# Where the Q, K and V columns are put in (dim, head) order: in the weights, or in the copy out of PSUM

## The chip, the core and the metric

The kernel runs on one NeuronCore of a Trainium2 chip. Its engines are TensorE (PE, matmuls and transposes into PSUM), VectorE (DVE), ScalarE (ACT), GpSimd (POOL) and SyncE (SP, which here only issues DMAs). Each engine runs its instructions in the order in which they were written for it, and waits for others by semaphores. The metric is the time of one execution in microseconds on the device.

## What is computed

One transformer block on 2048 positions of 576 columns, in bf16:

```
S, D, H, Dh, F = 2048, 576, 32, 18, 4608
y   = layernorm(x)                                   # no affine part, eps 1e-5
qkv = (y @ wqkv).reshape(S, 3, H, Dh)                # column = t*576 + head*18 + dim
q, k, v = qkv[:, 0], qkv[:, 1], qkv[:, 2]
idx = pos[:, None] - 2 * arange(8)                   # 8 earlier positions, two apart; masked below 0
logits[h, s, w] = dot(q[s, h], k[idx[s, w], h]) * 18 ** -0.5
attn = softmax(logits over w)
o[s, h] = sum over w of attn[h, s, w] * v[idx[s, w], h]
h1  = x + o.reshape(S, D) @ wo
out = h1 + gelu(layernorm(h1) @ w1 + b1) @ w2 + b2   # tanh form of gelu
```

## The kernel before

The positions are cut into 16 tiles so that partition p of tile j holds position 16 p + j. The eight keys that a query needs then lie in eight tiles of the same parity, and `ORDER` takes the even tiles first and the odd ones after, each from the highest down. `kwin[e]` and `vwin[e]` are windows of eight slots, one for each tile of parity e.

**Layout.** VectorE computes the scores: one product of the window with q (line 445), then sums over the 18 dims in halving steps (line 451), which need the columns in (dim, head) order, so that 32 heads lie next to each other. The weights come in (head, dim) order. In this kernel they are loaded as they are into a raw tile, `wraw` (lines 201 and 205, K by the ScalarE queue, V and Q by SP), and fifteen copies, `perm` (line 290), one for each of Q, K, V and each of the five blocks of 128 rows, put them into `wqkv_sb` in (dim, head) order. Blocks 1 and 3 are copied by ScalarE, blocks 0, 2 and 4 by VectorE. The queries, keys and values then leave TensorE in the wanted order.

**The first stage, for each tile n** (`front`): load x; statistics on VectorE (`ln1a`: lines 314, 315, and the variance with eps in line 318); the inverse root by a power on GpSimd (`ln1r`, line 322); normalisation (`ln1b`) on VectorE for the first eight tiles (line 354) and on ScalarE for the others (line 357, with a factor from GpSimd, line 349); transposition (`t1`), for the first eight tiles by TensorE (line 329) and a ScalarE copy out of PSUM (`t1e`, line 373), for the others by a transposing DMA (line 371). Then three chunks, `c{n}K`, `c{n}V`, `c{n}Q`: each ten matmuls (two halves of 288 columns, five blocks of rows, line 394) into one PSUM buffer of two banks, and one ScalarE copy, `e{n}K` and so on (line 406), into the window or a query tile. K chunks of the first eight tiles come first. The chunks of Q, K, V need all five `perm` copies of their third. The PSUM pool `pm` has three buffers, for transposes, chunks, projections and MLP units together.

**Attention and the rest.** VectorE needs eight K slots and a query for its first product (`p1a`), and all eight V slots for the weighted sum (line 486). Its outcome is transposed, projected by `wo` (line 564), added to x, normalised again, transposed again (`t2`, `t3`), and goes into the MLP, eight groups of two tiles: units of 36 matmuls with w1 (line 630), gelu on ScalarE (line 641), and matmuls with w2 (line 667). The last tiles' K and V slots are refilled, shifted by a row, through DRAM (lines 426, 427, 520, 522).

**Order.** All work is a list of tasks with an engine, an expected cost, tasks that they come after, a priority, and buffers that they take and give. A planner, `Weaver.run`, puts them in one order, always the task with the earliest start, by priority where starts tie; that fixes each engine's instruction order before the kernel runs. A changed cost or dependence can therefore reorder work far behind it. DMA tasks (`load`, `bulk`) carry a size; the planner holds bulk weights back while its model of the queue is full. The weights w2 (18 loads) wait for all `perm` copies, since their tile takes the place of `wraw`.

Of the kernel before, what the change touches and what calls it, by code (L numbers as in the profile page):

```python
# [8 lines left out]
ACT = mybir.ActivationFunctionType  # L9
ALU = mybir.AluOpType  # L10
AX = mybir.AxisListType
BF16 = mybir.dt.bfloat16
# [3 lines left out]
class Weaver:  # L16
# [74 lines left out]
def kernel(  # L91
# [46 lines left out]
    FH = FT // 2  # L138
    w1_sb = wpool.tile([P, KC, F // 2], BF16, name="w1_sb")
    wo_sb = wpool.tile([P, KC, HALF], BF16, name="wo_sb")  # L140
    hn_bufs = [wpool.tile([P, KC, 2 * P], BF16, name="hnT0")]
    b1_raw = wpool.tile([FT, P], BF16, name="b1_raw")
    b1_sb = wpool.tile([P, FT], F32, name="b1_sb")
    ident = wpool.tile([P, P], BF16, name="ident")
    b2_bc = wpool.tile([P, D], BF16, name="b2_bc")
# [7 lines left out]
    early_cm = tc.tile_pool(name="early", bufs=1)  # L153
    early = early_cm.__enter__()
    wqkv_sb = early.tile([P, KT, 3 * D], BF16, name="wqkv_sb")
    raw_cm = tc.tile_pool(name="raw", bufs=1, side="right")
    raw = raw_cm.__enter__()
    wraw = raw.tile([P, 3, KT, D], BF16, name="wraw")
    zrow = raw.tile([NT, 2 * D], BF16, name="zrow")

    late, w2p = {}, {}

    def late_pool():
        if not late:
# [24 lines left out]
    def bulk(name, fn, kb, after=(), prio=0.0, issue=0.45):  # L189
        add(name, "SP", issue, fn, after, prio, lag=2.0, kb=kb, backlog=SLACK)  # L190
# [6 lines left out]
    def wq_load(eng, t, k0, k1):  # L197
        def fn():
            src = bass.AP(tensor=A_wqkv.tensor, offset=A_wqkv[k0 * P, t * D].offset,
                          ap=[[3 * D, P], [P * 3 * D, k1 - k0], [1, D]])  # L200
            eng.dma_start(out=wraw[:, t, k0:k1, :], in_=src)
        return fn

    def wq_rest(eng, t):
        return lambda: eng.dma_start(out=wraw[0:64, t, 4, :], in_=A_wqkv[512:576, t * D:(t + 1) * D])

    def wo_load(half, dd):
        def fn():
# [15 lines left out]
        return fn  # L224

    def b1_load():
        nc.sync.dma_start(out=b1_raw[:], in_=B_b1.rearrange("(f p) -> f p", p=P))

    def w2_chunk(c):
        def fn():  # L230
            if "w2" not in w2p:
                raw_cm.__exit__(None, None, None)
                pool = ctx.enter_context(tc.tile_pool(name="w2p", bufs=1, side="right"))
                w2p["w2"] = pool.tile([P, FT, D], BF16, name="w2_sb")
            f0, f1 = c * FT // W2C, (c + 1) * FT // W2C
            nc.sync.dma_start(out=w2p["w2"][:, f0:f1, :],
                              in_=B_w2[f0 * P:f1 * P, :].rearrange("(ft p) c -> p ft c", p=P))
        return fn

# [14 lines left out]

    def b2_load():
        nc.sync.dma_start(out=b2_bc[:], in_=B_b2.partition_broadcast(P))
        nc.sync.dma_start(out=kvd[:, 0, :], in_=zrow[:])

    load("b2", b2_load, 150, prio=8.5, issue=0.7, transfers=2)
    load("b1", b1_load, 20, prio=9.0)  # L260
# [5 lines left out]
    for c in range(W1C):  # L266
        for half in range(2):
            for k in range(0, KC, W1K):
                bulk(f"w1{c}{half}{k}", w1_chunk(c, half, k), 295, prio=20 + c)
    perms = [f"perm{t}{kt}" for t in range(3) for kt in range(KT)]  # L270
    for c in range(W2C):
        bulk(f"w2{c}", w2_chunk(c), 295, prio=30 + c, after=perms + ["b2"])


    nc.gpsimd.memset(mhalf[:], -0.5)
# [1 line left out]
    nc.gpsimd.memset(T["x", 0][:, D:DP], 0.0)  # L277
    make_identity(nc, ident[:])
    nc.gpsimd.memset(wqkv_sb[64:128, KT - 1, :], 0.0)
    nc.gpsimd.memset(zrow[:], 0.0)  # L280
    for n in range(1, NT):
        nc.gpsimd.memset(T["x", n][:, D:DP], 0.0)

    for t in range(3):
        for kt in range(KT):
            def perm(t=t, kt=kt, on=None):
                rows = P if kt < KT - 1 else D - kt * P
                src = wraw[0:rows, t, kt, :].rearrange("p (h d) -> p d h", h=H, d=Dh)
                dst = wqkv_sb[0:rows, kt, t * D:(t + 1) * D].rearrange("p (d h) -> p d h", d=Dh, h=H)
                {"ACT": nc.scalar.copy, "DVE": nc.vector.tensor_copy}[on](out=dst, in_=src)  # L290
            on = "ACT" if kt in (1, 3) else "DVE"
            add(f"perm{t}{kt}", on, {"ACT": 1.23, "DVE": 0.65}[on], lambda f=perm, on=on: f(on=on),
                (f"W{t}{'aabbc'[kt]}",) + ((("ln1b0",) if kt == 2 else ()) if t == K else (f"t1e{2 + 2 * t}" if on == "ACT" else f"ln1b{W - 1}",)),
                prio=(-18, -100, -17)[t])

    def b1_turn():
        T["b1T"] = ps_pm.tile([P, 2048], BF16, tag="pm", name="b1T")[:, 0:FT]
        nc.tensor.transpose(T["b1T"], b1_raw[:], ident[0:FT, 0:FT])
# [22 lines left out]
    def ln_rstd(L, n):  # L321
        nc.gpsimd.tensor_tensor(out=L["rs"][:, n, :], in0=L["ve"][:, n, :], in1=mhalf[:], op=ALU.pow)  # L322
# [15 lines left out]
    def front(n):  # L338
# [2 lines left out]

        def ln1a():
            ln_stats(L1, n, T["x", n][:, 0:D])
            ln_var(nc.vector, L1, n, (1.0, EPS))

        def ln1r():
            ln_rstd(L1, n)
            if n >= W:
                nc.gpsimd.tensor_scalar(out=nmr[:, n, :], in0=L1["mv"][:, n, 0:1], scalar1=L1["rs"][:, n, :],
                                        scalar2=-1.0, op0=ALU.mult, op1=ALU.mult)  # L350
# [21 lines left out]
            else:  # L372
                nc.scalar.copy(out=T["xnT", n], in_=T["pt1", n])  # L373

        add(f"ln1a{n}", "DVE", 1.2, ln1a, (f"x{n}",) + (("ln1b0",) if n == 1 else ()), prio=-20 + n if n < W else 0.5 + (n - W) // 4)
        add(f"ln1r{n}", "POOL", 0.6 if n < W else 1.1, ln1r, (f"ln1a{n}",), prio=-20, lag=0.1 if n < W else 1.0)
        add(f"ln1b{n}", "DVE" if n < W else "ACT", 0.45 if n < W else 0.7, ln1b, (f"ln1r{n}",), prio=-20 + n)
        freed = [m for m in range(LENT, n) if n < 2 * LENT and region(m) == region(n)][-1:]
        room = [f"t1e{m}" for m in range(LENT) if not freed and LENT <= n < 2 * LENT]
# [4 lines left out]
        else:  # L384
            load(f"t1e{n}", lambda: t1e(True), 164, [f"ln1b{n}"] + room, prio=-20 + n, issue=1.2, lag=3.0)

        def chunk(t):
            def fn():
                pq = ps_pm.tile([P, 2, 512], F32, tag="pm", name="pq")
                T["pq", n, t] = pq  # L390
                for half in range(2):
                    c0 = t * D + half * HALF
                    for kt in range(KT):
                        nc.tensor.matmul(pq[:, half, 0:HALF], lhsT=T["xnT", n][:, kt, :],  # L394
                                         rhs=wqkv_sb[:, kt, c0:c0 + HALF],
                                         start=(kt == 0), stop=(kt == KT - 1))
            return fn

        def evict(t):
            def fn():  # L400
                if t == Q:
                    T["q", n] = wpool.tile([P, D], BF16, tag="q", name="q", bufs=NQ)
                    dst = T["q", n][:]
                else:
                    dst = (kwin if t == K else vwin)[e][:, s, :]
                nc.scalar.copy(out=dst.rearrange("p (a c) -> p a c", a=2), in_=T["pq", n, t][:, :, 0:HALF])  # L406
            return fn

        under = [m for m in range(LENT, min(n, 2 * LENT))
                 if region(m) * DP < (s + 1) * D and s * D < (region(m) + 1) * DP]  # L410
        for r, t in enumerate((K, V, Q)):
            first = t == K and n < W
            add(f"c{n}{'QKV'[t]}", "PE", 1.24, chunk(t), [f"t1e{n}"] + [f"perm{t}{kt}" for kt in range(KT)],
                prio=-50 + n if first else -25 if n == 0 and t == Q else -24 + n if t == V and n < W else -10 + n + 0.2 * r,
                take=("pm", f"pq{n}{t}"), lag=0.3)
            lent = []
            if e and t == K:
                lent = [f"t1e{m}" for m in range(LENT)] + [f"c{m}{c}" for m in under for c in "QKV"]
# [198 lines left out]
    def mlp(g):  # L617
# [39 lines left out]
        for i, (a, half) in enumerate(passes):  # L657
            n = ns[a]

            def piece(u, a=a, n=n, half=half):  # L660
                def fn():
                    if u == 0:
                        T["po", n, half] = ps_po.tile([P, HALF], F32, tag="po", name="po")
                    for q in range(2):
                        for r in range(2):
                            ft = r * FH + 2 * u + q
                            nc.tensor.matmul(T["po", n, half][:], lhsT=T["hT", g, u][:, r, q, a * P:(a + 1) * P],  # L667
                                             rhs=w2p["w2"][:, ft, half * HALF:(half + 1) * HALF],
                                             start=(u + q + r == 0), stop=(u == UN - 1 and q + r == 2))
                return fn  # L670

# [61 lines left out]
```

## Time and profile before

| | |
|---|---|
| median of 3 runs | 389.82 us (389.81 to 389.87) |
| profiled execution | 389.9 us, span 388.1 us |
| TensorE busy | 373.1 us, 96% of the span |
| VectorE busy | 297.1 us, 77% |
| ScalarE busy | 220.5 us, 57% |
| GpSimd busy | 37.2 us, 10% |
| clock granted to TensorE | 1.000 |

The times of the text are microseconds from the start of the span. A row of the timeline has start, duration, engine, line, operation, and what it writes and reads with partitions x elements; in square brackets how long the engine had been idle before it and what ended that. Merged rows end in the number of instructions, and their duration reaches from the start of the first to the end of the last.

### The profile page before, as it was taken

Reading aid. Unit: us, or ns where it says so; the run is one execution under the profiler, and the core shown is the slowest. Engines: PE = TensorE matmul, PEld = TensorE weight load, DVE = VectorE, ACT = ScalarE, POOL = GpSimd, SP = SyncE. Lnnn points to the kernel's source line nnn. Section 1 sums busy time; section 2 is a strip of 40 time slices with the busy share of each in tenths; the row PEclk is TensorE's granted clock in tenths of the full one; section 3 lists DMA queues with packets and bytes.
Section 4 is the critical chain, followed back from the end, with each engine's and each line's share of the span. In section 5 each row is a group of like instructions: output and inputs, shape, how many; then the busy total and the mean of one; then the engine's idle time right before and its main releaser. Section 6 shows DMA issues by size and latency. Waiting matters only on the chain.

```text
span 388.1 us, 10761 instructions
## 1 busy us (share of the span) xinstructions
PE 373.1 (96%) x4607; PEld 305.2 (79%) x4607; DVE 297.1 (77%) x559; ACT 220.5 (57%) x447; POOL 37.2 (10%) x65
## 2 busy tenths in 40 slices
PE   2889999999899999999999999999999999999996
PEld 1667877788777887887788878887888788778875
DVE  5999999999999999999999998989976952000000
ACT  4697767688914974188227823790487068306700
POOL 6455010101001000001100010110011011000000
PEclk9999999999999999999999999999999999999999
DMA  8988899887232402127333214222312432100000
GB/s 264 277 165 227 213 212 272 254 255 235 57 83 51 105 19 61 33 63 63 70 77 73 61 48 94 63 47 76 78 37 43 108 64 21 29 15 19 2 15 17
DMA packets 63968, 38.48 MB, mean 99 GB/s; under 512 B 39520, under 2 KB 63904, under 8 KB 63920
## 3 DMA queue, kind: packets, MB, share of 16 engines
q1 hardware_dynamic: 63296, 37.13, 40.4%
q8 instruction: 36, 0.59, 0.7%
q10 hardware_dynamic: 624, 0.66, 0.5%
q14 instruction: 12, 0.10, 0.1%
HBM read 22.28 MB, written 6.52 MB: 74 GB/s over the span
## 4 chain that ended last, share of the span: by engine, by line
PE 74%; DVE 12%; issue 1%; ACT 1%; DVEq 0%; ACTq 0%
PE po L667 37%; PE pm L630 33%; PE pw L564 4%; DVE prod L445 3%; DVE prod L451 2%; DVE prod L486 1%; ACT hT L641 1%; DVE prod L492 1%; DVE l_st L314 1%; DVE h L577 1%; DVE hb L590 1%; DVE half L438 0%; DVE prod L496 0%; DVE half L439 0%; DVE lg L458 0%
## 5 line engine op out<-in xcount | busy, mean ns | idle before, releaser
L641 ACT ACTIVATE hT<-pm,b_sb 128x256 bf16<-128x256 f32 x288 | 111.9, 482 | 82.1 <-PE pm L630 81.8
L630 PE MATMUL pm<-hnT,w_sb 64*128 64x256 bf16 x2592 | 144.5, 269 | 0.8 <-ACT hT L641 0.8
L667 PE MATMUL po<-w_sb,hT 128*128 128x288 bf16 x1152 | 143.2, 286 | 0.0
L630 PEld LDWEIGHTS <-w_sb 64*128 64x128 bf16 x2592 | 125.9, 94 | 17.7 <-issue 2.4
L667 PEld LDWEIGHTS <-hT 128*128 128x128 bf16 x1152 | 111.7, 98 | 30.6 <-issue 2.4
L686 DVE TENSOR_TENSOR osb<-po,hb 128x288 bf16<-128x288 f32 x32 | 14.4, 453 | 57.1 <-PE po L667 57.1
L322 POOL TENSOR_TENSOR l_rs<-l_ve,mhalf 128x1 f32<-128x1 f32 x32 | 28.4, 888 | 287.8 <-DVE l_ve L318 287.8
L451 DVE TENSOR_TENSOR prod<-prod 128x2304 bf16<-128x2304 bf16 (+1 forms) x64 | 44.2, 690 | 1.8
L486 DVE TENSOR_TENSOR prod<-vwin,at 128x4608 bf16<-128x4608 bf16 x16 | 40.9, 2554 | 0.4
L445 DVE TENSOR_TENSOR prod<-kwin,q 128x4608 bf16<-128x4608 bf16 x16 | 40.9, 2555 | 0.3
L394 PE MATMUL pq<-wqkv_sb,vwin 128*128 128x288 bf16 x210 | 30.1, 303 | 3.2 <-ACT vwin L373 1.8
L594 ACT ACTIVATE hn<-h,nmr,l_rs 128x576 bf16<-128x576 f32 (+1 forms) x32 | 19.2, 651 | 23.0 <-issue 11.6
L394 PEld LDWEIGHTS <-vwin 128*128 128x128 bf16 x210 | 21.2, 103 | 10.5 <-ACT vwin L373 2.6
L394 PE MATMUL pq<-wqkv_sb,kwin 128*128 128x288 bf16 x210 | 27.2, 286 | 0.0
L394 PEld LDWEIGHTS <-kwin 128*128 128x128 bf16 x210 | 20.3, 98 | 5.4 <-issue 0.5
L492 DVE TENSOR_TENSOR prod<-prod 128x2304 bf16<-128x2304 bf16 x16 | 21.7, 1358 | 0.6
L569 ACT COPY h<-pw 128x576 f32<-128x576 f32 x16 | 10.4, 651 | 19.4 <-PE pw L564 19.4
L564 PE MATMUL pw<-wo_sb,oT 64*128 64x288 bf16 x288 | 20.3, 283 | 0.0
L577 DVE TENSOR_TENSOR h<-h,xr 128x576 f32<-128x576 f32 x16 | 12.0, 752 | 9.6 <-ACT h L569 9.6
L564 PEld LDWEIGHTS <-oT 64*128 64x128 bf16 x288 | 13.5, 94 | 4.5 <-issue 1.4
L406 ACT CAST kwin<-pq 128x576 bf16<-128x576 f32 x16 | 10.2, 648 | 8.5 <-PE pq L394 8.3
L314 DVE BATCH_NORM_STATS2 l_st<-h 128x6 f32<-128x288 f32 x32 | 13.1, 452 | 0.6
(62 smaller groups left out, 238.2 us busy)
## 6 DMA issues: line engine op xcount, KB each, us to landing
w_sb<-in_B_w_dram SPq DMA_DIRECT2D x36, 288.0 KB, 4.7
xr<-in_A_x_dram SPq DMA_DIRECT2D x16, 144.0 KB, 2.3
out_dram<-osb SPq DMA_DIRECT2D x16, 144.0 KB, 1.8
kvd<-kwin SPq DMA_DIRECT2D x14, 144.0 KB, 4.1
kvd<-vwin SPq DMA_DIRECT2D x14, 144.0 KB, 3.7
kwin<-kvd SPq DMA_DIRECT2D x14, 144.0 KB, 2.5
vwin<-kvd SPq DMA_DIRECT2D x14, 144.0 KB, 2.1
wraw<-in_A_wqkv_dram SPq DMA_DIRECT2D x4, 288.0 KB, 4.1
```

Source lines behind the costliest of these rows:

```text
L314: nc.vector.bn_stats(out=st[:, c, :], in_=src[:, c * HALF:(c + 1) * HALF])
L322: nc.gpsimd.tensor_tensor(out=L["rs"][:, n, :], in0=L["ve"][:, n, :], in1=mhalf[:], op=ALU.pow)
L394: nc.tensor.matmul(pq[:, half, 0:HALF], lhsT=T["xnT", n][:, kt, :], rhs=wqkv_sb[:, kt, c0:c0 + HALF], start=(kt == 0), stop=(kt == KT - 1))
L445: nc.vector.tensor_tensor(out=prod[:], in0=kwin[e][:], in1=T["q", n][:].unsqueeze(1).to_broadcast([P, W, D]), op=ALU.mult)
L451: nc.vector.tensor_tensor(out=pv[:, :, 0:b - a, :], in0=pv[:, :, 0:b - a, :], in1=pv[:, :, a:b, :], op=ALU.add)
L486: nc.vector.tensor_tensor(out=prod[:].rearrange("p w (d h) -> p w d h", d=Dh, h=H), in0=vwin[e][:].rearrange("p w (d h) -> p w d h", d=Dh, ...
L492: nc.vector.tensor_tensor(out=prod[:, 0:4, :], in0=prod[:, 0:4, :], in1=prod[:, 4:8, :], op=ALU.add)
L564: nc.tensor.matmul(pw[:, half, 0:HALF], lhsT=T["oT", n][lo:lo + 64, block(c, half), :], rhs=wo_sb[lo:lo + 64, c, :], start=(c == 0), stop= ...
L594: nc.scalar.activation(out=hn_slots[n % 2][:, c0:c1], in_=src, func=ACT.Identity, scale=L2["rs"][:, n, :], bias=nmr[:, n, :])
L630: nc.tensor.matmul(pm[:, half, q, 0:width], lhsT=w1_sb[lo:lo + 64, c, f0:f0 + P], rhs=T["hnT", g][lo:lo + 64, block(c, half), 0:width], st ...
L641: nc.scalar.activation(out=T["hT", g, u][:, half, q, 0:width], in_=T["pm", g, u][:, half, q, 0:width], func=ACT.Gelu_apprx_tanh, bias=b1_s ...
L667: nc.tensor.matmul(T["po", n, half][:], lhsT=T["hT", g, u][:, r, q, a * P:(a + 1) * P], rhs=w2p["w2"][:, ft, half * HALF:(half + 1) * HALF ...
```

## The change

The weights are loaded straight into `wqkv_sb` in (head, dim) order, and the fifteen `perm` copies and `wraw` are gone. The eviction of each chunk now puts the columns from (head, dim) to (dim, head). For that the PSUM buffer of a chunk is laid out so that its two halves meet at the border of the two banks, and the 576 results lie next to each other. Q and K are evicted in the order of the destination, so ScalarE reads PSUM in steps of 18 fp32 elements (72 bytes) and writes contiguously. V is evicted in the order of the source: ScalarE reads contiguously and writes in steps of 32 bf16 elements (64 bytes).

Along with it: the variance of the first eight tiles moves from VectorE's `ln1a` into GpSimd's `ln1r`, with the planner's costs of both changed; the tile of w2 exists from the start, and lends its room to the raw b1 and to a row of zeros, so w2 now waits for their readers in place of the `perm` copies. The expected cost of an eviction stays 0.68.

```diff
+    w2_sb = wpool.tile([P, FT, D], BF16, name="w2_sb")
+    b1_raw = w2_sb[0:FT, 2, 0:P]
-    b1_raw = wpool.tile([FT, P], BF16, name="b1_raw")
...
-    wraw = raw.tile([P, 3, KT, D], BF16, name="wraw")
-    zrow = raw.tile([NT, 2 * D], BF16, name="zrow")
...
-            eng.dma_start(out=wraw[:, t, k0:k1, :], in_=src)
+            eng.dma_start(out=wqkv_sb[:, k0:k1, t * D:(t + 1) * D], in_=src)
...
-        return lambda: eng.dma_start(out=wraw[0:64, t, 4, :], in_=A_wqkv[512:576, t * D:(t + 1) * D])
+        return lambda: eng.dma_start(out=wqkv_sb[0:64, 4, t * D:(t + 1) * D], in_=A_wqkv[512:576, t * D:(t + 1) * D])
...
-            if "w2" not in w2p:
-                raw_cm.__exit__(None, None, None)
-                pool = ctx.enter_context(tc.tile_pool(name="w2p", bufs=1, side="right"))
-                w2p["w2"] = pool.tile([P, FT, D], BF16, name="w2_sb")
...
-        nc.sync.dma_start(out=kvd[:, 0, :], in_=zrow[:])
+        nc.sync.dma_start(out=kvd[:, 0, :], in_=w2_sb[0:NT, 0:2, :].rearrange("p a c -> p (a c)"))
...
-    perms = [f"perm{t}{kt}" for t in range(3) for kt in range(KT)]
     for c in range(W2C):
-        bulk(f"w2{c}", w2_chunk(c), 295, prio=30 + c, after=perms + ["b2"])
+        bulk(f"w2{c}", w2_chunk(c), 295, prio=30 + c, after=("b2", "b1t"))
...
-    nc.gpsimd.memset(zrow[:], 0.0)
+    nc.gpsimd.memset(w2_sb[0:NT, 0:2, :], 0.0)
...
-    for t in range(3):
-        for kt in range(KT):
-            def perm(t=t, kt=kt, on=None):
-                rows = P if kt < KT - 1 else D - kt * P
-                src = wraw[0:rows, t, kt, :].rearrange("p (h d) -> p d h", h=H, d=Dh)
-                dst = wqkv_sb[0:rows, kt, t * D:(t + 1) * D].rearrange("p (d h) -> p d h", d=Dh, h=H)
-                {"ACT": nc.scalar.copy, "DVE": nc.vector.tensor_copy}[on](out=dst, in_=src)
-            on = "ACT" if kt in (1, 3) else "DVE"
-            add(f"perm{t}{kt}", on, {"ACT": 1.23, "DVE": 0.65}[on], lambda f=perm, on=on: f(on=on), ...
...
         def ln1a():
             ln_stats(L1, n, T["x", n][:, 0:D])
-            ln_var(nc.vector, L1, n, (1.0, EPS))
+            if n >= W:
+                ln_var(nc.vector, L1, n, (1.0, EPS))

         def ln1r():
+            if n < W:
+                ln_var(nc.gpsimd, L1, n, (1.0, EPS))
             ln_rstd(L1, n)
...
-        add(f"ln1a{n}", "DVE", 1.2, ln1a, ...
-        add(f"ln1r{n}", "POOL", 0.6 if n < W else 1.1, ln1r, ...
+        add(f"ln1a{n}", "DVE", 1.07 if n < W else 1.2, ln1a, ...
+        add(f"ln1r{n}", "POOL", 0.95 if n < W else 1.1, ln1r, ...
...
         def chunk(t):
             def fn():
-                pq = ps_pm.tile([P, 2, 512], F32, tag="pm", name="pq")
+                pq = ps_pm.tile([P, 1024], F32, tag="pm", name="pq")
                 T["pq", n, t] = pq
                 for half in range(2):
                     c0 = t * D + half * HALF
+                    p0 = 512 - HALF + half * HALF
                     for kt in range(KT):
-                        nc.tensor.matmul(pq[:, half, 0:HALF], lhsT=T["xnT", n][:, kt, :],
+                        nc.tensor.matmul(pq[:, p0:p0 + HALF], lhsT=T["xnT", n][:, kt, :],
                                          rhs=wqkv_sb[:, kt, c0:c0 + HALF],
                                          start=(kt == 0), stop=(kt == KT - 1))
...
-                nc.scalar.copy(out=dst.rearrange("p (a c) -> p a c", a=2), in_=T["pq", n, t][:, :, 0:HALF])
+                src = T["pq", n, t][:, 512 - HALF:512 + HALF].rearrange("p (h d) -> p h d", h=H)
+                dst = dst.rearrange("p (d h) -> p h d", h=H)
+                if t != V:
+                    src, dst = (ap.rearrange("p h d -> p d h") for ap in (src, dst))
+                nc.scalar.copy(out=dst, in_=src)
...
-            add(f"c{n}{'QKV'[t]}", "PE", 1.24, chunk(t), [f"t1e{n}"] + [f"perm{t}{kt}" for kt in range(KT)],
+            add(f"c{n}{'QKV'[t]}", "PE", 1.24, chunk(t), [f"t1e{n}"] + [f"W{t}{part}" for part in "abc"],
```

More of the change, by code (lines that the diff above doesn't have):

```diff
@@ L155 @@
     wqkv_sb = early.tile([P, KT, 3 * D], BF16, name="wqkv_sb")
-    raw_cm = tc.tile_pool(name="raw", bufs=1, side="right")
-    raw = raw_cm.__enter__()
-    wraw = raw.tile([P, 3, KT, D], BF16, name="wraw")
-    zrow = raw.tile([NT, 2 * D], BF16, name="zrow")
-    late, w2p = {}, {}
+    late = {}
     def late_pool():
@@ L226, in b1_load @@
     def b1_load():
-        nc.sync.dma_start(out=b1_raw[:], in_=B_b1.rearrange("(f p) -> f p", p=P))
+        nc.sync.dma_start(out=b1_raw, in_=B_b1.rearrange("(f p) -> f p", p=P))
     def w2_chunk(c):
         def fn():
-            if "w2" not in w2p:
-                raw_cm.__exit__(None, None, None)
-                pool = ctx.enter_context(tc.tile_pool(name="w2p", bufs=1, side="right"))
-                w2p["w2"] = pool.tile([P, FT, D], BF16, name="w2_sb")
             f0, f1 = c * FT // W2C, (c + 1) * FT // W2C
-            nc.sync.dma_start(out=w2p["w2"][:, f0:f1, :],
+            nc.sync.dma_start(out=w2_sb[:, f0:f1, :],
                               in_=B_w2[f0 * P:f1 * P, :].rearrange("(ft p) c -> p ft c", p=P))
@@ L279 @@
     nc.gpsimd.memset(wqkv_sb[64:128, KT - 1, :], 0.0)
-    nc.gpsimd.memset(zrow[:], 0.0)
+    nc.gpsimd.memset(w2_sb[0:NT, 0:2, :], 0.0)
     for n in range(1, NT):
         nc.gpsimd.memset(T["x", n][:, D:DP], 0.0)
-    for t in range(3):
-        for kt in range(KT):
-            def perm(t=t, kt=kt, on=None):
-                rows = P if kt < KT - 1 else D - kt * P
-                src = wraw[0:rows, t, kt, :].rearrange("p (h d) -> p d h", h=H, d=Dh)
-                dst = wqkv_sb[0:rows, kt, t * D:(t + 1) * D].rearrange("p (d h) -> p d h", d=Dh, h=H)
-                {"ACT": nc.scalar.copy, "DVE": nc.vector.tensor_copy}[on](out=dst, in_=src)
-            on = "ACT" if kt in (1, 3) else "DVE"
-            add(f"perm{t}{kt}", on, {"ACT": 1.23, "DVE": 0.65}[on], lambda f=perm, on=on: f(on=on),
-                (f"W{t}{'aabbc'[kt]}",) + ((("ln1b0",) if kt == 2 else ()) if t == K else (f"t1e{2 + 2 * t}" if on == "ACT" else f"ln1b{W - 1}",)),
-                prio=(-18, -100, -17)[t])
     def b1_turn():
         T["b1T"] = ps_pm.tile([P, 2048], BF16, tag="pm", name="b1T")[:, 0:FT]
-        nc.tensor.transpose(T["b1T"], b1_raw[:], ident[0:FT, 0:FT])
+        nc.tensor.transpose(T["b1T"], b1_raw, ident[0:FT, 0:FT])
     add("b1t", "PE", 0.1, b1_turn, ("b1",), prio=-35, take=("pm", "b1t"), lag=0.3)
@@ L373, in t1e @@
                 nc.scalar.copy(out=T["xnT", n], in_=T["pt1", n])
-        add(f"ln1a{n}", "DVE", 1.2, ln1a, (f"x{n}",) + (("ln1b0",) if n == 1 else ()), prio=-20 + n if n < W else 0.5 + (n - W) // 4)
-        add(f"ln1r{n}", "POOL", 0.6 if n < W else 1.1, ln1r, (f"ln1a{n}",), prio=-20, lag=0.1 if n < W else 1.0)
+        add(f"ln1a{n}", "DVE", 1.07 if n < W else 1.2, ln1a, (f"x{n}",) + (("ln1b0",) if n == 1 else ()), prio=-20 + n if n < W else 0.5 + (n - W) // 4)
+        add(f"ln1r{n}", "POOL", 0.95 if n < W else 1.1, ln1r, (f"ln1a{n}",), prio=-20, lag=0.1 if n < W else 1.0)
         add(f"ln1b{n}", "DVE" if n < W else "ACT", 0.45 if n < W else 0.7, ln1b, (f"ln1r{n}",), prio=-20 + n)
@@ L667, in fn @@
                             nc.tensor.matmul(T["po", n, half][:], lhsT=T["hT", g, u][:, r, q, a * P:(a + 1) * P],
-                                             rhs=w2p["w2"][:, ft, half * HALF:(half + 1) * HALF],
+                                             rhs=w2_sb[:, ft, half * HALF:(half + 1) * HALF],
                                              start=(u + q + r == 0), stop=(u == UN - 1 and q + r == 2))
```

## The prediction

> **What bounds the kernel now.** I read the page's busy shares first, then the slices, then windows of the stage that the change touches.
>
> ```profile
> PE 373.1 (96%) x4607; PEld 305.2 (79%) x4607; DVE 297.1 (77%) x559; ACT 220.5 (57%) x447; POOL 37.2 (10%) x65
> ...
> PE   2889999999899999999999999999999999999996
> ...
> ACT  4697767688914974188227823790487068306700
> ```
>
> TensorE works in nearly every slice; its only thin one is the first. The span is TensorE's work plus the little that it loses, so an edit that leaves its instructions alone (this one does) acts only through TensorE's idle or slow stretches: it can shorten those of the head, or make new ones.
>
> The stage in question is Q, K, V: 48 chunks of ten matmuls, each evicted by ScalarE. The windows show TensorE and ScalarE from the end of the head to the last eviction, and in the burst of eight V chunks. Columns: window, length, then busy time (instructions) of PE, PEld, DVE, ACT, POOL, then clock, DMA share, GB/s.
>
> ```profile
> 28.83:82.70 53.87, 53.20 (x479) 41.87 (x478) 51.37 (x87) 38.11 (x61) 7.45 (x8) 1.00 0.96 240
> ...
> 28.83:39.00 10.17, 9.89 (x81) 7.68 (x79) 9.65 (x22) 8.20 (x15) 5.14 (x5) 1.00 0.84 229
> ```
>
> TensorE idles 0.67 us in 53.87; ScalarE has 15.76 us free. That spare time pays for dearer evictions, and no more: until 82 us TensorE has only these chunks and a few projections to run.
>
> The head, from the timeline (start us, us, engine, line):
>
> ```profile
> 6.71 0.72 PE L329 MATMUL pt<-ident,kwin 128*128 128x128 bf16 x5 [6.71 <-DVE kwin L354]
> ...
> 8.21 2.58 PE L394 MATMUL pq<-wqkv_sb,vwin 128*128 128x288 bf16 x10 [0.79 <-ACT vwin L373]
> ...
> 12.12 2.58 PE L394 MATMUL pq<-wqkv_sb,vwin 128*128 128x288 bf16 x10 [0.79 <-ACT vwin L373]
> ...
> 14.50 1.27 PE L329 MATMUL pt<-ident,kwin 128*128 128x128 bf16 x10
> ...
> 16.03 1.68 PE L394 MATMUL pq<-wqkv_sb,vwin 128*128 128x288 bf16 x10 [0.26 <-ACT vwin L373]
> ...
> 19.55 3.64 DVE L290 COPY wqkv_sb<-wraw 128x576 bf16<-128x576 bf16 x6
> ...
> 22.24 1.26 ACT L290 COPY wqkv_sb<-wraw 128x576 bf16<-128x576 bf16 x1
> ...
> 23.37 0.72 ACT L373 COPY kwin<-pt 128x640 bf16<-128x640 bf16 x1
> ...
> 24.14 1.39 PE L394 MATMUL pq<-wqkv_sb,vwin 128*128 128x288 bf16 x10 [0.95 <-ACT kwin L373]
> ...
> 26.59 7.61 PE L394 MATMUL pq<-wqkv_sb,vwin 128*128 128x288 bf16 x60
> ```
>
> A chunk takes 2.58 us at 8 and 12 us and 1.22 later (24.14 to 25.37, say, is 1.23 start to start). The weight copy at 22.24 holds ScalarE while the transposes of tile 7 wait, and TensorE waits for their copy at 23.37. From 26.59 chunks run without a gap.
>
> The prices (min/median/max in ns):
>
> ```profile
> L290 DVE COPY wqkv_sb<-wraw x9: 658/678/684, 4.8 to 22.5; 128x576 bf16<-128x576 bf16 x6, 64x576 bf16<-64x576 bf16 x3
> L290 ACT COPY wqkv_sb<-wraw x6: 1218/1244/1270, 4.4 to 24.5; 128x576 bf16<-128x576 bf16 x6
> ...
> L406 ACT CAST vwin<-pq x16: 619/639/695, 29.5 to 80.3; 128x576 bf16<-128x576 f32 x16
> ...
> L349 POOL TENSOR_SCALAR nmr<-l_mv,l_rs x8: 267/268/1115, 20.4 to 39.2; 128x1 f32<-128x1 f32 x8
> ```
>
> **Removed.** Six permuting copies on ScalarE, 6 x 1.24 = 7.5 us, and nine on VectorE, 9 x 0.68 = 6.1 us, all before 26 us. Most stood beside other work; the two at 22.24 and 24.49 stood on TensorE's path.
>
> **Moved.** For the first eight tiles the variance step goes from VectorE (0.15 us) to GpSimd. There it costs 0.27 us by the shortest L349 row, or 1.1 when VectorE copies run beside it; in the changed order only statistics do, as beside the short rows. For tile 0 nothing covers it: GpSimd was still clearing x at 5.68, so VectorE's variance was free, and now about 0.35 us (0.27 and a 0.1 gap) stands before the first normalisation and TensorE's start. For later tiles VectorE takes the next tile's statistics first, about 1.0 us, which cover it. Two 9- and 36-KB helpers (raw b1, the zero row) move into the tile of w2, which only makes w2 wait for their readers.
>
> **Queues.** SP: in the changed order two transposing loads of tiles 8 and 10 stand ahead of all w1 loads, each waiting for a normalisation on ScalarE, so SP holds w1 back by some us. w1 is first read at 81.95, its last load went out at 66.35 before; w2's last went out at 93.2 and its first reader ran at 103.25, with 4.7 us to landing. So 5 us are covered; past that, each us late costs one. The K weights come on the ScalarE queue as before, and GpSimd clears the same bytes.
>
> **Head, summed.** TensorE starts at 6.71 + 0.35 = 7.05, the first chunk at 8.55, slow, to 11.1. The transposes of tiles 1 and 2 now both follow (0.74 each), so the second chunk starts at about 12.45 and ends near 15.0; one set of transposes is left instead of two, and the third chunk starts at 15.5 instead of 16.03, at 1.5 us for a half-recovered pace. Then a tile is 1.50 (17.83 to 19.33): chunks at 17.35, 18.85, 20.35. Then Q of tile 0 at 21.6, transposes, the last two K chunks at 23.1 and 24.4, and V starts at 25.7. Before, the same work was done at 26.59 + 1.22 = 27.8. Gain 2.1 us; everything behind it, VectorE's first score product included (28.92, waiting for this Q), moves up with it. Bounds: one more chunk at the slow pace takes 1.36 back, one fewer gives 1.4: 0.7 to 3.5.
>
> **The 48 evictions.** No row shows ScalarE reading PSUM at a stride of 72 bytes (Q, K) or writing SBUF at a stride of 64 bytes (V). Below, the contiguous eviction, 0.64; above, ScalarE's permuting copy, 1.24; cheaper than contiguous is excluded, since every element is still moved. I take 0.64. For Q and K that row shares engine, source memory, type and count; the 1.24 row shares the order but reads another memory. The stride alone is not dear: VectorE pays 0.68 for the very copy that costs ScalarE 1.24. And PSUM is faster than ScalarE: TensorE puts 288 columns there in 0.122 us, 2.4 per ns, while ScalarE takes 576 in 0.53 (75.25 to 75.77 start to start), 1.1 per ns, so one element at a time should leave it fed (an estimate: writing is not reading). For V the nearest row on writing is the projection's eviction, which writes twice the bytes at 0.651 against 0.639; what a stride does there is open.
>
> A rule speaks against this choice. The Trainium skill (SBUF — State Buffer, Specifications) gives SBUF 16-byte lines and PSUM 8-byte lines, and wants at least two hits per line for full speed. ScalarE's 1.24 against 0.64 agrees with it; no row shows it for PSUM reads or SBUF writes. By the rule all 48 evictions are slow, and the time is that of the first rival; by my choice it is that of the forecast.
>
> **Sum.** The profiled execution took 389.9 (span 388.1 and 1.8 around it), 0.08 over the median of 389.82. 389.9 - 2.1 = 387.8. Its own range is 386.0 to 389.4: the head's bounds, and about 0.4 either way for the start of the MLP, where TensorE idles 1.57 us of 82 to 103 and the order changes.
>
> **Rivals.** *Both strides cost 1.24* (slower). 39 evictions in 28.83:82.70 gain 0.60 each: 38.11 + 23.4 = 61.5 against 53.87, 7.6 over. In the head ScalarE needs seven transposed copies, nine evictions and three normalisations (4.9 + 11.2 + 2.8 = 18.9) from 11.1 on, to 30.0 instead of 28.83; the third normalisation, 0.9, leaves the window. 389.9 + 7.6 + 1.2 - 0.9 = 397.8, less up to 1 that TensorE runs ahead through its PSUM buffers: 397 (393 if evictions overlap their neighbours by 0.1 each). It decides once 39 evictions outgrow 15.76 us, above 1.04 us each. For it: the 1.24 row. Against: another source memory.
>
> *One direction costs it.* V alone: the burst needs 8.20 + 8 x 0.60 = 13.0 in 10.17, 2.8 lost, the rest fits: 387.8 + 2.8 = 390.6. Q and K alone: 38.11 + 23 x 0.60 = 51.9 of 53.87, and the head's gain is gone: about 391.5. Together 391.
>
> *The head does not move*: the copies were hidden and the slow chunks set its pace, 0.35 lost at the start and little regained: 389.8. For it: only about 1 us of TensorE's waits there names a copy held up by a permutation.
>
> **How the numbers follow.** Forecast 0.50, both slow 0.27, one direction 0.15, no gain 0.08. What a measurement can tell from no change is 0.2%, 0.78 us. Faster: 0.47 of the forecast and 0.02 of one direction, 0.49; same: 0.03, 0.07 and 0.02, 0.12; slower 0.39. The range 386.0 to 397.0 holds nearly all of the forecast, both middle cases and half of the first rival.
>
> **What will show it.** The eviction's median: 0.64 to 0.7 for the forecast, near 1.24 for the rival; above 1.04 TensorE must show idle time ended by ScalarE's evictions. TensorE should start near 7.05, V chunks near 25.7, the last Q chunk about 2 us before 81.95. A price between the ends, an earlier recovery of TensorE's pace, or late w1 loads would make me wrong.

## The result

The changed kernel takes 408.36 us (median of 4, 407.73 to 409.01) against 389.82 before: 18.5 us longer, ratio 1.0475 (95% interval 1.0457 to 1.0494). The forecast was 387.8, with a range up to 397.0. The profiled execution took 408.38, span 406.6.

The page of the changed kernel, first its busy shares and then its slices:

```profile
PE 377.5 (93%) x4607; PEld 307.6 (76%) x4607; DVE 290.4 (71%) x542; ACT 242.5 (60%) x441; POOL 33.4 (8%) x73
...
PE   2977698878979999999999999999999999999996
...
ACT  1699969899993568417823880585079228504710
...
PEclk9996899999999999999999999999999999999999
```

From the third slice to the tenth, but for the sixth, ScalarE is now at 8 or 9 and TensorE at 6 to 8, where it stood at 8 or 9 before. In the fourth slice and the fifth TensorE's clock is also granted at 0.6 and 0.8. Of the 18.5 us, TensorE's idle time makes 14.1 (406.6 - 377.5 = 29.1 against 388.1 - 373.1 = 15.0) and its longer busy time 4.4, for the same 4607 matmuls.

The evictions, by tile (duration in ns, min/median/max), and the time that TensorE's chunks waited (us, times), all of it for evictions of V:

```profile
L396 ACT CAST kwin<-pq x16: 611/638/986, 10.9 to 95.5; 128x576 bf16<-128x576 f32 x16
L396 ACT CAST q<-pq x16: 617/638/1036, 21.6 to 99.5; 128x576 bf16<-128x576 f32 x16
L396 ACT CAST vwin<-pq x16: 2687/2712/3071, 26.0 to 97.3; 128x576 bf16<-128x576 f32 x16
...
  PE pq L380: 12.7, 12
```

This is the whole case in three rows. Reading PSUM in steps of 72 bytes costs nothing: K and Q take 0.638 us as before. Writing SBUF in steps of 64 bytes costs V 2.71, four times the contiguous price and more than twice the dearest that I had thought possible.

TensorE's timeline where the V chunks begin:

```profile
23.03 1.40 PE L380 MATMUL pq<-wqkv_sb,kwin 128*128 128x288 bf16 x10
24.26 2.61 PE L380 MATMUL pq<-wqkv_sb,vwin 128*128 128x288 bf16 x20
28.81 1.39 PE L380 MATMUL pq<-wqkv_sb,vwin 128*128 128x288 bf16 x10 [1.93 <-ACT vwin L396]
31.86 2.56 PE L380 MATMUL pq<-wqkv_sb,vwin 128*128 128x288 bf16 x10 [1.67 <-ACT vwin L396]
34.90 2.56 PE L380 MATMUL pq<-wqkv_sb,vwin 128*128 128x288 bf16 x10 [0.48 <-ACT vwin L396]
```

V starts at 24.26, earlier than the 27.8 of before and than the 25.7 that I forecast: the head did gain. Two V chunks later TensorE waits for a PSUM buffer, 1.93 and 1.67 us before the next two chunks, and after these two waits a chunk takes 2.56 instead of 1.39: from 30.2 to 34.0 us the granted clock is 0.56 in the mean. The slow pace adds little to these three chunks: they start 3.05 and 3.04 us apart, the fast one and the slow ones alike, as ScalarE frees the buffers, and a slow chunk shortens the next wait, to 0.48.

### The profile page after: what moved, and what is told of

Read it like the earlier page. It is cut to its first block, busy times and chain, and to the rows that moved or that the text cites. A ratio compares the mean times of both kernels' runs of the same rounds, so it can differ in the third digit from the quotient of the medians.

```text
span 406.6 us, 10742 instructions
## 1 busy us (share of the span) xinstructions
PE 377.5 (93%) x4607; PEld 307.6 (76%) x4607; DVE 290.4 (71%) x542; ACT 242.5 (60%) x441; POOL 33.4 (8%) x73
## 4 chain that ended last, share of the span: by engine, by line
PE 79%; ACT 16%; issue 3%; POOL 1%; DVE 0%; POOLq 0%; ACTq 0%
PE po L657 35%; PE pm L620 32%; ACT vwin L396 8%; PE pq L380 8%; PE pw L554 4%; ACT hT L631 2%; ACT L631 1%; PE pt L309 1%; ACT hn L584 1%; ACT x L340 1%; ACT kwin L396 1%; ACT L458 1%; POOL wqkv_sb L271 0%; ACT vwin L356 0%; ACT hnT L340 0%
## 5 line engine op out<-in xcount | busy, mean ns | idle before, releaser
L620 PEld LDWEIGHTS <-w_sb 64*128 64x128 bf16 x2592 | 127.5, 94 | 18.9 <-issue 5.3
L302 POOL TENSOR_TENSOR l_rs<-l_ve,mhalf 128x1 f32<-128x1 f32 x32 | 24.8, 775 | 307.9 <-DVE l_ve L298 307.3
L396 ACT CAST vwin<-pq 128x576 bf16<-128x576 f32 x16 | 42.8, 2767 | 3.0 <-PE pq L380 3.0
L380 PE MATMUL pq<-wqkv_sb,vwin 128*128 128x288 bf16 x210 | 33.8, 322 | 9.2 <-ACT vwin L396 7.7
L380 PEld LDWEIGHTS <-vwin 128*128 128x128 bf16 x210 | 22.4, 109 | 18.9 <-issue 9.7
L428 DVE TENSOR_TENSOR half<-lg 128x128 f32<-128x128 f32 x32 | 9.2, 289 | 19.8 <-ACT lg L458 19.3
```

The source lines that it names most:

```text
L380: nc.tensor.matmul(pq[:, p0:p0 + HALF], lhsT=T["xnT", n][:, kt, :], rhs=wqkv_sb[:, kt, c0:c0 + HALF], start=(kt == 0), stop=(kt == KT - 1))
L396: nc.scalar.copy(out=dst, in_=src)
L620: nc.tensor.matmul(pm[:, half, q, 0:width], lhsT=w1_sb[lo:lo + 64, c, f0:f0 + P], rhs=T["hnT", g][lo:lo + 64, block(c, half), 0:width], st ...
```

## The experiments

**One direction for all.** The one thing undone is V's direction:

```diff
-                if t != V:
-                    src, dst = (ap.rearrange("p h d -> p d h") for ap in (src, dst))
+                src, dst = (ap.rearrange("p h d -> p d h") for ap in (src, dst))
```

> The changed kernel with one thing undone: V is evicted in the order of the destination, as Q and K are, so ScalarE reads PSUM in steps of 72 bytes and writes contiguously; nothing writes SBUF in steps any more. Theory A (the price lies in ScalarE's stepped writes of SBUF alone: 2.71 us for each of 16 V evictions): V's evictions fall to 0.64, TensorE no longer waits for them, and only the shorter head is left. In the changed kernel V chunks begin at 25.5 at the latest (they began at 24.3) against 27.8 before, so 389.8 less 2.3 to 3.5: 386.3 to 387.5, faster than before. Theory B (V's evictions are slow because of what runs beside them in the stage, or TensorE is held by the new order and the later w1 loads): evictions of V stay above 1 us or TensorE's gaps stay, and the time is above 390.

387.54 us (387.34 to 388.36) against 389.95 beside it, ratio 0.9944 (0.9932 to 0.9956). Theory A holds: this edit alone takes back 20.8 us and makes the kernel faster than before. Its evictions, and a window of the V burst (window, length, busy time and instructions of PE, PEld, DVE, ACT, POOL, then clock, DMA share, GB/s):

```profile
L395 ACT CAST vwin<-pq x16: 622/638/667, 25.6 to 76.4; 128x576 bf16<-128x576 f32 x16
...
25.50:45.00 19.50, 19.50 (x171) 15.30 (x170) 18.62 (x27) 14.40 (x24) 0.81 (x2) 1.00 0.96 237
```

The same window of the changed kernel:

```profile
25.50:45.00 19.50, 13.20 (x82) 8.75 (x80) 9.40 (x19) 19.50 (x13) 0.81 (x2) 0.82 0.59 159
```

With stepped writes ScalarE is busy for all of 19.50 us and gets 13 instructions done, TensorE 82 matmuls at a mean clock of 0.82; with stepped reads ScalarE does 24 in 14.40 and TensorE 171 matmuls without a gap.

**The directions exchanged.** Q and K now write in steps, V reads in steps:

```diff
-                if t != V:
+                if t == V:
```

> The changed kernel with the two orders exchanged: Q and K are evicted with contiguous reads and writes in steps of 64 bytes, V with stepped reads. Theory A (the direction sets the price, whichever tile it is): 32 evictions near 2.71 and V's near 0.64; ScalarE gets 32 x 2.07 = 66 us more. In the changed kernel 16 x 2.07 = 33 us more cost about 22 over what the head should have given, so some 11 were absorbed; here 66 - 11 = 55 us over 386 to 387: about 441, 430 to 450. Theory B (it is V's window, or what runs beside V's evictions): Q and K stay under 1 us and the time is under 395.

One execution, 435.66 us, in the range of theory A. Q and K now take 2.70 and 2.72, V 0.645: the price goes with the direction and not with V's tile, its place in the order or its neighbours.

**Copies by themselves.** Behind the last gelu, ScalarE and VectorE make single copies of 128x576, with a view of the destination or the source that steps (`b` is a bf16 slot of the dead V window, `f` an fp32 tile, `ps` PSUM):

```diff
+            nc.scalar.copy(out=view(b, 2), in_=ps)      # steps of 4 bytes; then 4, 8, 16, 18, 32, 36, 64
+            nc.scalar.copy(out=b, in_=view(ps, 18))     # stepped read of PSUM
+            nc.scalar.copy(out=view(f, 16), in_=ps)     # fp32 in steps of 64 bytes
+            nc.vector.tensor_copy(out=view(b, 32), in_=ps)
```

> The first kernel of this set with single copies of 128x576 added behind the last gelu, where ScalarE and VectorE are idle and no DMA but the last stores runs; their results are not used. Written in steps of 4, 8, 16, 32, 36, 64, 72 and 128 bytes, read from PSUM in steps of 72 and 256 bytes, from SBUF in steps of 36 and 64 bytes, fp32 written in steps of 64 bytes, and four of them on VectorE. Theory A (a stepped write costs ScalarE by itself): the 64-byte write takes 2.7 us here too, from PSUM and from SBUF. Theory B (company in the stage): it takes under 1.3. If the size of a step matters by lines of SBUF, steps of 4 and 8 bytes cost near 0.64 and all from 16 or 32 on the same; if by banks that powers of two hit again and again, 36 and 72 bytes are cheaper than 32, 64 and 128. If it is the two-byte element, the fp32 write in steps of 64 bytes takes near 0.65. Stepped reads of PSUM: 0.64 at both steps. VectorE: about 0.7 for every form, since its stepped copy of the weights took 0.68. The time: that of the first run, up to 3 us more for VectorE's copies in the tail.

The rows of these copies, in the order of the text above (lines 703 to 711 write bf16 contiguously and in steps of 4, 8, 16, 32, 36, 64, 72 and 128 bytes; 712 and 713 read PSUM in steps of 72 and 256; 714 writes fp32 in steps of 64; 716 and 717 read SBUF in steps of 64 and 36; 721 and 722 are VectorE writing in steps of 64 and reading PSUM in steps of 72):

```profile
L703 ACT CAST vwin<-pz x2: 639/647/655, 366.8 to 393.8; 128x576 bf16<-128x576 f32 x2
L704 ACT CAST vwin<-pz x2: 797/800/802, 367.4 to 394.5; 128x576 bf16<-128x576 f32 x2
L705 ACT CAST vwin<-pz x2: 1431/1437/1443, 368.3 to 395.3; 128x576 bf16<-128x576 f32 x2
L706 ACT CAST vwin<-pz x2: 2702/2716/2729, 369.7 to 396.8; 128x576 bf16<-128x576 f32 x2
...
L709 ACT CAST vwin<-pz x2: 2650/2650/2650, 377.8 to 404.8; 128x576 bf16<-128x576 f32 x2
L710 ACT CAST vwin<-pz x2: 2613/2613/2613, 380.5 to 407.5; 128x576 bf16<-128x576 f32 x2
...
L712 ACT CAST vwin<-pz x2: 639/639/639, 385.9 to 412.9; 128x576 bf16<-128x576 f32 x2
L713 ACT CAST vwin<-pz x2: 639/639/639, 386.5 to 413.5; 128x576 bf16<-128x576 f32 x2
L714 ACT COPY fz<-pz x2: 1126/1126/1126, 387.1 to 414.1; 128x576 f32<-128x576 f32 x2
...
L716 ACT COPY vwin<-vwin x2: 1154/1154/1154, 390.7 to 417.7; 128x576 bf16<-128x576 bf16 x2
L717 ACT COPY vwin<-vwin x2: 1212/1212/1212, 391.9 to 418.9; 128x576 bf16<-128x576 bf16 x2
...
L721 DVE CAST vwin<-pz x2: 2648/2648/2648, 421.6 to 427.4; 128x576 bf16<-128x576 f32 x2
L722 DVE CAST vwin<-pz x2: 758/758/758, 424.3 to 430.0; 128x576 bf16<-128x576 f32 x2
```

Theory A: the 64-byte write takes 2.65 with no company, and 2.70 from SBUF (line 715). The price does not single out powers of two (2.61 at 72 bytes), which ends the bank theory. It nearly doubles from 4 to 8 to 16 bytes and then stays. The line theory has the second half of that, but it wanted 0.64 at 4 and 8 bytes, which take 0.80 and 1.44; and fp32 elements at 64 bytes take 1.13, which fits neither that theory at one price nor the two-byte theory's 0.65. I missed VectorE: it pays 2.65 for the stepped write from PSUM and 1.41 from SBUF, not 0.7. I missed the time too: 448.35, since VectorE's copies wait for ScalarE's and the last outputs stand behind them on VectorE.

**Runs of elements.** What was left open was whether a line or a lone element costs. Copies from PSUM behind the last output, now with runs of 2, 4, 8 and 16 elements at steps of 64 bytes (lines 710 to 713), fp32 contiguous and in steps of 8, 16 and 72 bytes (714 to 717), and fp32 in pairs (718):

```diff
+            nc.scalar.copy(out=runs(b, 16, 2), in_=flat(ps, 16, 2))   # pairs of bf16, 64 bytes apart
+            nc.scalar.copy(out=runs(f, 8, 2), in_=flat(ps, 8, 2))     # pairs of fp32, 64 bytes apart
```

> The kernel with V's reads stepped, with copies of 576 elements on ScalarE from PSUM added behind the last output, where nothing else runs; their results are not used. In the earlier set bf16 steps of 4, 8 and 16 bytes took 0.80, 1.44 and 2.72 and larger steps 2.6, and fp32 in steps of 64 bytes 1.13. Theory L (each 16-byte line that a write touches costs 4.4 ns when elements are bf16, and steps of 4 and 8 bytes put 4 and 2 elements into a line): bf16 in runs of 2, 4, 8 and 16 elements at steps of 64 bytes touches 288, 144, 72 and 72 lines: 1.44, 0.80, 0.65, 0.65; fp32 in steps of 8 bytes 288 lines of its own price, 0.65, in steps of 16 and 72 bytes 1.13. Theory W (a two-byte element that isn't written together with its neighbour in the same four-byte word is what costs): runs of 2 already take 0.65. The whole run ends later by the copies, about 26 us, so 413.

```profile
L709 ACT CAST vwin<-pz x2: 2649/2649/2649, 385.6 to 395.9; 128x576 bf16<-128x576 f32 x2
L710 ACT CAST vwin<-pz x2: 640/640/641, 388.3 to 398.6; 128x576 bf16<-128x576 f32 x2
...
L715 ACT COPY fz<-pz x2: 664/664/665, 391.5 to 401.8; 128x576 f32<-128x576 f32 x2
L716 ACT COPY fz<-pz x2: 1167/1167/1167, 392.2 to 402.5; 128x576 f32<-128x576 f32 x2
L717 ACT COPY fz<-pz x2: 1235/1237/1239, 393.4 to 403.7; 128x576 f32<-128x576 f32 x2
L718 ACT COPY fz<-pz x2: 642/642/642, 394.7 to 405.0; 128x576 f32<-128x576 f32 x2
```

Pairs of bf16 64 bytes apart cost 0.640, as much as a contiguous write (runs of 4, 8 and 16 cost 0.64 too); theory L wanted 1.44. So what is dear is a bf16 element written without its neighbour. Theory W is right on the pairs but not whole: it has no reason for 0.80, 1.44 and 2.72 in steps of 4, 8 and 16 bytes, where every element is alone, and fp32 elements alone at 16 bytes or more also cost 1.13 to 1.24, and in pairs 0.642. Which mechanism sets the price of a lone element stays open. The whole took 408.21, not 413.

**Was it the plan?** The planner of the changed kernel counts 0.68 for an eviction of V. Told better:

```diff
-            add(f"e{n}{'QKV'[t]}", "ACT", 0.68, evict(t), ...
+            add(f"e{n}{'QKV'[t]}", "ACT", 2.2 if t == V else 0.68, evict(t), ...
```

> The changed kernel (408.4) with the planner told 2.2 us for an eviction of V in place of 0.68; the evictions themselves are untouched. Theory A (ScalarE has more work than the stage has room for: 16 x 2.07 = 33 us more against 15.8 free before): no order hides it, V's evictions still take 2.7, and the time is 400 to 408. Rival (the false cost in the plan made most of the loss): under 396.

One execution, 404.1 us, in the range of theory A, V still at 2.715. An honest cost gives back 4 of 18.5 us, and the rest stays in this order. That no other order gives more back is not shown: from 25.5 to 100 us ScalarE is busy for 67.9 of 74.5 us here.

**The moved variance.** First with the planner's costs moved back too, then without:

```diff
             ln_stats(L1, n, T["x", n][:, 0:D])
-            if n >= W:
-                ln_var(nc.vector, L1, n, (1.0, EPS))
+            ln_var(nc.vector, L1, n, (1.0, EPS))

         def ln1r():
-            if n < W:
-                ln_var(nc.gpsimd, L1, n, (1.0, EPS))
...
-        add(f"ln1a{n}", "DVE", 1.07 if n < W else 1.2, ln1a, ...     # first run only
-        add(f"ln1r{n}", "POOL", 0.95 if n < W else 1.1, ln1r, ...
+        add(f"ln1a{n}", "DVE", 1.2, ln1a, ...
+        add(f"ln1r{n}", "POOL", 0.6 if n < W else 1.1, ln1r, ...
```

> The run above with the variance of the first eight tiles back on VectorE and the planner's costs of that step as before. The prediction charged 0.35 us for the move at TensorE's start; the changed kernel's trace shows the start only 0.03 later, and normalisations 1.27 apart in place of 1.50, while TensorE takes 1.50 for a tile. Theory A (TensorE's own pace sets the head, the move is worth nothing): within 0.4 us of the run above. Rival (VectorE's pace sets it): normalisations again 1.50 apart, and 1 to 2 us slower than the run above.

390.51 us (390.48 to 393.02), ratio to before 1.0032 (1.0018 to 1.0047): 3.0 slower than the run with V's reads stepped, more than either theory had. So I kept the order and moved only the work:

> As the run with V's reads stepped (387.5), with the variance of the first eight tiles done by VectorE, but with the planner's costs left as they are there, so that every engine's order is the same. The run that moved the variance back with its costs took 390.5: its TensorE began 0.4 earlier, but its order took one transpose, then a chunk, then one transpose, where the faster run has two transposes ahead of the second chunk, and its chunks stayed slow (2.58, 2.58, 2.23 against 2.58, 1.60, 1.39). Theory O (the order, and with it TensorE's early pace, made the 3 us): this run recovers its pace as the faster one does and stands within 0.6 of it, 387.0 to 388.2. Theory P (VectorE's longer pace made it): normalisations again 1.50 apart, V chunks begin 1 to 2 us later than at 23.8, and the time is 388.5 to 390.5.

387.13 us (387.11 to 387.20), ratio 0.9928 (0.9916 to 0.9940), the fastest of all. VectorE's normalisations are 1.50 apart again, and it does not matter. The 3 us come with the order that other planned costs make, not with the place of the variance. That TensorE's early pace makes all of them, as theory O has it, is not shown: in the two profiled executions V chunks begin 2.8 us apart (26.0 and 23.2), but the spans differ by 5.7 (391.0 and 385.3), so half of the difference is lost behind the head. TensorE's rows of the two runs, first with the costs moved back (this profiled execution took 392.74, one of its longer ones):

```profile
7.83 2.58 PE L377 MATMUL pq<-wqkv_sb,vwin 128*128 128x288 bf16 x10 [0.78 <-ACT vwin L353]
10.21 0.74 PE L309 MATMUL pt<-ident,kwin 128*128 128x128 bf16 x5
11.74 2.58 PE L377 MATMUL pq<-wqkv_sb,vwin 128*128 128x288 bf16 x10 [0.79 <-ACT vwin L353]
```

and with the order kept:

```profile
7.84 2.58 PE L377 MATMUL pq<-wqkv_sb,vwin 128*128 128x288 bf16 x10 [0.78 <-ACT vwin L353]
10.21 1.27 PE L309 MATMUL pt<-ident,kwin 128*128 128x128 bf16 x10
11.75 1.40 PE L377 MATMUL pq<-wqkv_sb,vwin 128*128 128x288 bf16 x10 [0.26 <-ACT vwin L353]
```

Both reach the second chunk at the same time. Behind one set of transposes and a pause of 0.79 us the chunk runs at the slow pace, behind two sets and a pause of 0.26 at full pace. It looks as if the shorter pause were the cause; the next run speaks against it.

**The move in the kernel before.** The permuting copies and contiguous evictions are kept; only the move and its costs are taken from the change:

```diff
-            ln_var(nc.vector, L1, n, (1.0, EPS))
+            if n >= W:
+                ln_var(nc.vector, L1, n, (1.0, EPS))

         def ln1r():
+            if n < W:
+                ln_var(nc.gpsimd, L1, n, (1.0, EPS))
```

> The kernel before, permuting copies and contiguous evictions kept, with only the variance of the first eight tiles moved to GpSimd and the planner's costs of that step changed as in the changed kernel. If the move is worth 3 us by itself, as between the two runs without stepped writes: about 387. If it gains only where the copies are gone (they stand between VectorE's steps and on ScalarE): 389 to 390.5, no difference or a little slower, for TensorE's start comes 0.4 later. The clock of the early chunks tells: if they recover by the second chunk the first holds.

390.06 us (388.87 to 390.70), ratio 0.9993 (0.9983 to 1.0004): no difference. The profiled execution, 388.88, began at 7.12 instead of 6.71 and recovered its pace by the second chunk, so the sign that I had named for the first theory shows there, yet the median has no gain. Its executions lie at two levels, near 388.9 and near 390.1; whether the upper ones recover later was not profiled.

```profile
12.52 1.40 PE L397 MATMUL pq<-wqkv_sb,vwin 128*128 128x288 bf16 x10 [0.79 <-ACT vwin L376]
```

This second chunk follows one set of transposes and a pause of 0.79 us, and yet runs at full pace. And with the same order and the same pause of 0.26 the second chunk took 2.08 us in the changed kernel, 1.60 with V's reads stepped and 1.40 with VectorE's variance. So the pause does not decide the pace. What does stays open: the granted clock reads 1.00 in the windows of all these chunks.

**Where the head's gain went.** In the run with V's reads stepped, V chunks begin at 23.78, 4.0 us before the 27.8 of the kernel before, but the span is only 2.3 shorter. I tried to get the rest back by holding two exponentials together:

```diff
-        gate = [...] if g >= 3 else [f"p1b{n}"]
+        gate = [...] if g >= 2 else [f"p1b{n}"]
```

> As the run with V's reads stepped (387.5), with the exponentials of tiles 4 and 5 both held until the last gelu of the first MLP group, as the kernel does for later groups. In that run V chunks begin 4.0 us earlier than before, but the end comes only 2.3 earlier; TensorE idles 3.1 of 80 to 104 against 1.6 of 82 to 103 before, waiting for gelus, while ScalarE is busy 22.4 of 24 and loads tables six times around three exponentials. If those loads are where the gain goes, a pair less (2.6 us of ScalarE) gives back 0.5 to 1.5: 386.0 to 387.0. Rival: the attention of tiles 4 and 5 gets late for its projections and TensorE waits elsewhere: 387.5 or more.

389.43 us (389.20 to 390.18): the rival holds. Windows of the run with V's reads stepped, then of this one:

```profile
80.00:104.00 24.00, 20.86 (x341) 18.50 (x337) 22.44 (x41) 22.38 (x46) 0.99 (x1) 1.00 0.65 199
104.00:125.00 21.00, 20.63 (x218) 15.96 (x216) 19.94 (x39) 7.78 (x13) 1.99 (x2) 1.00 0.29 71
```

```profile
80.00:104.00 24.00, 22.25 (x351) 19.61 (x345) 22.51 (x38) 21.23 (x45) 0.99 (x1) 1.00 0.66 198
104.00:125.00 21.00, 19.84 (x221) 16.43 (x223) 19.92 (x42) 6.09 (x13) 0.99 (x1) 1.00 0.20 43
```

TensorE's idle time of 80 to 104 falls from 3.1 to 1.75 us, as hoped; 104 to 125 then loses 1.2 instead of 0.4, and 125 to 300, which had no gap, loses 2.2. The place is so shown: 1.9 us of the head's gain (3.5 us idle of 80 to 125 against 1.6 of 82 to 125 before) are given back where the MLP starts and TensorE waits for gelus on a ScalarE that is busy 22.4 of 24 us. A cure was not found.

## Why the prediction was wrong

**The step that failed** is the price of V's 16 evictions: 0.64 in the sum, and "above, ScalarE's permuting copy, 1.24" as the end of the range for V as well. That row is a stepped read of SBUF. For a stepped write the text itself found no row ("what a stride does there is open"), and then took 1.24 as the ceiling all the same. It is 2.71. The other support, that the stride alone is not dear since VectorE pays 0.68 for the weight copy, is a stepped read again: VectorE's stepped write takes 2.65 from PSUM. A ceiling borrowed from another kind of access is no ceiling, and a path that no row shows deserved a wider range than two near rows give.

**Q and K: the price was right.** 0.638 at 72 bytes in the kernel, 0.639 at 72 and 256 in the copies by themselves. The reason given, that PSUM delivers faster than ScalarE takes, agrees with this and was not tested apart.

**The rule that spoke against it.** The Trainium skill (SBUF — State Buffer, Specifications) wants at least two hits per 16-byte line of SBUF, and gives PSUM lines of 8 bytes. For ScalarE's stepped reads of SBUF the copies agree (1.21 at 36 bytes, 1.15 at 64). Read in the same way for ScalarE's reads of PSUM, as my prediction did, the rule fails: 0.639. For writes it is right in part: one bf16 element to a line is dear (2.57 to 2.72), pairs 64 bytes apart, two to a line, are not (0.640), and fp32 costs 0.66 in steps of 8 bytes and 1.17 in steps of 16. But bf16 in steps of 8 bytes also puts two elements into a line, and costs 1.44. So hits per line alone do not set the price of a write. Weighing one rule for both directions hid that they are two questions.

**The rivals.** *One direction costs it* named the mechanism and the place, V's burst of eight chunks. Its working with the measured price: 8.20 + 8 x 2.07 = 24.8 in 10.17, 14.6 over; behind it 8 x 2.07 = 16.6 against 13.8 free, 2.8 over; less the head's 3.5, 389.9 + 13.9 = 403.8. The measured 408.4 is 4.6 more, and the loss does not lie where this working puts it. Windows of the changed kernel, from the first V chunk to the end of the burst, and from there to the first matmul with w1:

```profile
24.26:48.26 24.00, 15.83 (x103) 10.71 (x100) 9.49 (x20) 24.00 (x17) 1.26 (x4) 0.85 0.56 150
48.26:100.01 51.75, 44.85 (x389) 33.54 (x389) 44.75 (x72) 43.47 (x45) 1.98 (x2) 0.97 0.86 207
```

In the burst ScalarE has no free moment and TensorE idles 8.2 us. Behind it TensorE idles 6.9 us, where the working has 2.8, although ScalarE is free for 8.3 us of that window. Free time summed over a stage does not help if it is not there when TensorE waits for a buffer. The other term that the working lacks is the clock (0.85 and 0.97 in these windows), with TensorE's busy time 4.4 us longer over the whole span; how the 4.6 divide between the two is not shown. *Both strides* and *no gain* did not happen.

**The head.** The charge for the variance on GpSimd, 0.35, was about right: TensorE starts at 6.74 with it and at 6.34 with the same order and VectorE's variance. I forecast 7.05, since I did not see that GpSimd's clearing of x, which was running beside a VectorE copy of weights at 4.76, would end sooner without it (it takes 0.57 us now, and 0.95 both before and in the run that moved the variance and kept the copies). The gain was underrated: V at 25.7 forecast, 24.26 measured, 23.78 in the run with V's reads stepped. Of the 1.44 us, 0.31 are the start, 0.50 the second chunk, which I left at the slow pace of 2.58 and which took 2.08, and 0.34 the time from the third chunk to the fourth (1.85 forecast, 1.51 measured); the rest lies in smaller steps. The run with V's reads stepped is 0.48 earlier still, since its second chunk took 1.60. Why the pace recovered so early is open, as said. Two slips of the text changed little: of the two copies that it puts on TensorE's path only that at 22.24 held TensorE, whose rows have no gap from 24.14 to 34.2; and the forecast's own upper bound adds up to 389.6, not 389.4.

**The MLP's start**, given as 0.4 either way, took 1.9 us of the gain. With the evictions all in the cheap direction the time is 387.54, near my 387.8, but by luck, through two errors that cancel: 4.0 gained where I had 2.1, and 1.9 given back where the sum had nothing. The loads of w1, the other doubt, cost nothing: no wait of TensorE names them.

## What to carry to other kernels

In this kernel a permutation in an eviction is free or ruinous by which side steps: let ScalarE read PSUM in steps (72 and 256 bytes were free) and write contiguously, or in runs of two elements at least (shown at 64 bytes). When an operation's price is bounded by "the nearest row", check that the row steps on the same side, of the same memory; if none does, the upper end is unknown. And where TensorE is the bound and another engine has spare time, the price at which that spare time ends (here 1.04 us for an eviction) should be compared with the worst case, not with the expected one; and it should be counted where the waits fall, since here TensorE idled 6.9 us beside 8.3 us of ScalarE's free time.

## What the runs showed of the hardware

For 576 elements in each partition, in us:

| access | ScalarE | VectorE |
|---|---|---|
| PSUM read in steps of 72 bytes, contiguous write | 0.64 | 0.76 |
| contiguous PSUM read, contiguous write | 0.64 | 0.76 |
| SBUF read in steps of 36 bytes (bf16), contiguous write | 1.21 | 0.68 (the weight copies) |
| bf16 write in steps of 4, 8, 16 bytes | 0.80, 1.44, 2.72 | not run |
| bf16 write in steps of 32 to 128 bytes | 2.57 to 2.72 | 2.65 (64 bytes) |
| bf16 pairs, 64 bytes apart | 0.64 | not run |
| fp32 write in steps of 8 bytes, or in pairs 64 bytes apart | 0.66, 0.64 | not run |
| fp32 write in steps of 16 to 72 bytes | 1.13 to 1.24 | not run |

The V eviction's price hardly depends on company: 2.71 in the busy stage and 2.65 alone. And TensorE's clock was granted at 0.82 in the mean over 25.5 to 45 us, where it was idle for no more than 1.9 us at a time but for a third of the whole.
